# A two-channel convolution beside attention: filter rows loaded one row and one channel per DMA, ten row slots in a ring

## The chip, the cores and the metric

The kernel runs on one core of one Trainium2 chip. A core has a matrix engine (TensorE, PE in the profile, its weight loads PEld), a vector engine (VectorE, DVE), a scalar engine (ScalarE, ACT), GpSimd (POOL) and SyncE (SP), which here does nothing but issue DMAs. Sixteen DMA engines serve the queues of all of them. The metric is the device time of one execution in microseconds (us), lower is better.

## The reference

Two independent blocks share one output of 2048 rows and 1024 columns, in bf16. Block A (columns 0 to 511) is multi-head attention with 32 heads of 16; block B (columns 512 to 1023) is a long convolution over 2048 time steps, a filter for each of 512 channels, between two products.

```
def _A_ref(x, wqkv, wo):                      # x (1, 2048, 512), 32 heads
    qkv = (x @ wqkv) -> q, k, v
    p = softmax(q k^T * 16**-0.5)
    return (p v) @ wo

def _B_ref(q, k, v, shift_k, ssm_k, ssm_D):   # each (1, 2048, 512); ssm_k (512, 2048)
    k_shift = 4-tap causal filter of k along time, by channel
    kv = k_shift * v
    y = causal convolution of kv with ssm_k along time, by channel (there through an FFT)
    y = y + kv * ssm_D
    return q * y

return concatenate([a, b], axis=-1)
```

## The kernel before, in words

The program is written out engine by engine: a planner in Python keeps a time for each engine, takes the next piece of work that fits, and appends instructions to the five engines' lists with the semaphores that each must wait for. Nothing is reordered after that. The backbone is attention in steps T: `emit_qk` puts two or three blocks of scores into PSUM (L546), ScalarE takes their exponential (L557), some blocks go to VectorE instead (L593 to L605), and `pv_step` multiplies the results by V (L639) two steps later. Between these, `emit_bg` fills TensorE's free time with projections and with the convolution.

The convolution runs over 64 octets of channels (`NOCT`), `od` in the code, and an octet over 32 lags (`NLAG`). A lag is four matmuls (L814), one for each pair of channels: the pair's row `c` of the octet holds one channel on partitions 0 to 63 and the other on partitions 64 to 127. The moving operand is a slice of `WR`, ten slots of 128 partitions by 2048 elements. What stands there is a filter row read at a shifting start: partition p of a half takes 2048 elements from element p on of that channel's row, so that one stored row of `kz_scratch` (a padded, reversed copy of the filters in device memory) fills 64 partitions with 4 KB each.

`load_wr` fills the slots, in SP's queue, whenever slots are free. `wr_free` is the list of free slots with the handle that frees each; `wr_slot[x]` tells where item `x` went; `h_wr[x]` is the handle of its landing. Before the change an item is a pair of neighbouring rows in a pair of slots (five pairs, semaphores `d_wr0` to `d_wr4`), and its two halves are loaded by two DMAs of 64 partitions x 2 rows x 2048 elements, 512 KB each. An octet uses two items. At the last lag of an octet `conv_lags` returns its slots and calls `load_wr`, so SP waits there for a matmul (`s_pe`) and then issues the loads of an octet in one go. Six slots are filled at first, after the store of `kz_scratch` (`kz_store`); the other four hold V for the products of k and v until those are done. `emit_bg` starts an octet only when its rows have landed by the planner's reckoning (400 KB a us, 3.6 us ahead of the first).

Of the kernel before, what the change touches and what calls it, by code (L numbers as in the profile page):

```python
# [11 lines left out]
S = 2048  # L12
# [122 lines left out]
def bass_concat_heads__mha_block__ssm_conv_h3__prompt_kernel(  # L135
# [125 lines left out]
    d_outB = [DmaSem(sem(f"d_outB{i}")) for i in range(2)]  # L261
    d_outE = DmaSem(sem("d_outE"))
    d_outA = [DmaSem(sem(f"d_outA{i}")) for i in range(R_A)]
    d_wr = [DmaSem(sem(f"d_wr{i}")) for i in range(R_W // 2)]


    wview = A_wqkv.rearrange("(c p) f -> p c f", p=128)
# [111 lines left out]
    def evac_unit(u, bank, h):  # L379
        kind = u[0]  # L380
        if kind == "q":
            _, qb, o = u
            for par in range(2):
                hh = h_q[(qb, 2 * o + par)] = urgent(
                    lambda e, par=par: e.tensor_scalar(QT[:, qb % 2, 2 * o + par, :], PS[:, bank, :], MASK[:, par:par + 1], None, ALU.mult),  # L385
                    [h, h_mask] + ([h_kzt[0], h_kvm[0]] if qb == 1 else []), us=V512)
        elif kind == "k":
            _, o, sc = u
            c0 = KEYS0 if (o, sc) == (0, 0) else 0
            hh = urgent(lambda e: e.tensor_copy(KTo[:, o, sc * 512 + c0:(sc + 1) * 512], PS[:, bank, c0:512]), [h],  # L390
                        us=(0.335, 0.46) if c0 else V512)
            h_k[(o, sc)] = hh
        elif kind == "kv":
            _, c, i = u
            for p in range(2):
                dst = KV[64 * p:64 * p + 64, i // 4, 4 * (i % 4):4 * (i % 4) + 4, p, 32 * c:32 * c + 32, :].rearrange("p e k c -> p k e c")
                val = VST[64 * p:64 * p + 64, c, i // 4, 4 * (i % 4):4 * (i % 4) + 4, :].rearrange("p e (k c) -> p k e c", c=4)
                src = PS[64 * p:64 * p + 64, bank, :].rearrange("p (e k c) -> p k e c", e=4, c=4)
                h_kvc[c] = hh = urgent(lambda e, dst=dst, src=src, val=val: e.tensor_tensor(dst, src, val, ALU.mult),  # L399
                                       [h, h_vn[2 * c + i // 4], h_kv0], us=V512)  # L400
            kv_n[c] += 1
            if c == 0 and kv_n[0] == 8:
                load_qn(0, [h])
            if sum(kv_n) == 16:
                h_kvm[0] = h
                wr_free.extend([(3, hh), (4, hh)])
                load_wr()
        else:
            _, kt = u
            dst = VAF[:, kt, 0:H * VW].rearrange("p (h e) -> p h e", e=VW)[:, :, 0:DH]  # L410
            src = PS[:, bank, :].rearrange("p (h e) -> p h e", h=H)
            hh = urgent(lambda e: e.tensor_copy(dst, src), [h, h_vaf1], us=V512)  # L412
            h_v[kt] = hh
        bank_free[bank] = hh
# [22 lines left out]
    def kz_store(us):  # L437
        h = dve.op(lambda e: e.tensor_tensor(KZS[:, :, S - 1:S], KZS[:, :, S - 1:S], DSS, ALU.add), [h_kzt[0]], us=us)
        h_kzw[0] = dma(sp, d_kzw, kz_ap.rearrange("(p c) m -> p c m", c=4), KZS, [h, h_kz0], kb=2176)
        load_kt(1, h_kzt[0])  # L440
        wr_free.extend([(i, h_kzw[0]) for i in range(3)])
        load_wr()

    def make_dg(us):
# [339 lines left out]
    wr_slot = {}  # L784

    def load_wr():
        while wr_free and wr_next[0] < 2 * NOCT:
            (i, dep), x = wr_free.pop(0), wr_next[0]
            wr_next[0] += 1
            wr_slot[x] = i  # L790
            for h in range(2):
                row = 256 * (x // NOCT) + 128 * h + 2 * (x % NOCT)
                src = bass.AP(tensor=kz_ap.tensor, offset=kz_ap[row, 0].offset, ap=[[1, 64], [LKZ, 2], [1, S]])
                h_wr[x] = dma(sp, d_wr[i], WR[64 * h:64 * h + 64, 2 * i:2 * i + 2, :], src, [h_kzw[0], dep])

    def load_qn(i, deps):
        h_qn[i] = dma(pool, d_q[0], QN[:, :, :],
# [1 line left out]

    def conv_lags(od, n0, n1):  # L800
        kk = od % 4
        deps = [h_wr[2 * od], h_wr[2 * od + 1], h_kvc[2 * od // NOCT]]
        rows = [2 * wr_slot[2 * od + c // 2] + c % 2 for c in range(4)]
        if kk == 0 and n0 == 0:
            deps.append(bank_free[BGB])

# [12 lines left out]
        h = pe.op(fn, deps, us=(0.06 + 0.055 * (n1 - n0), 0.46 + 0.055 * (n1 - n0)),  # L819
                  run=0.054 * (n1 - n0))  # L820
        if n1 == NLAG:
            wr_free.extend([(wr_slot[2 * od], h), (wr_slot[2 * od + 1], h)])
            load_wr()
            if kk == 3:
                src = PS[:, BGB, :]
                src = bass.AP(tensor=src.tensor, offset=PS[:, BGB, 127:128].offset,
                              ap=[src.ap[0], [128, 4], [-1, 128]])
                hh = urgent(lambda e: e.tensor_copy(YB[:, :].rearrange("p (k i) -> p k i", k=4), src),
                            [h, h_yb.get(od // 4 - 1)], slack=0.3, us=V512)
                bank_free[BGB] = h_ybw[od // 4] = hh  # L830
# [123 lines left out]
    def emit_bg(T):  # L954
# [154 lines left out]
```

## Time and profile before

| | us |
|---|---|
| median of 2 runs | 979.33 |
| lowest, highest | 978.06, 980.59 |
| the profiled execution | 979.65 |
| its span, first to last instruction | 977.8 |

The profiled execution's time is 1.85 us over its span; what lies around the span is not in the trace. Busy shares are averages over a span with three stages: an opening of some 200 us with loads and projections, a middle in which attention and convolution run side by side, and an end after the last octet at 950 us.

### The profile page before, as it was taken

To read this page: it belongs to the slowest core of one execution; us is meant where nothing else is said; L and a number is where in the kernel's file an instruction comes from. 1 tells how busy PE (TensorE), PEld (TensorE's weight loads), DVE (VectorE), ACT (ScalarE), POOL (GpSimd) and SP (SyncE) were. 2 spreads that over 40 slices of the span, in tenths; PEclk is the share of its full clock that TensorE was granted. 3 is DMA by queue.
4 is the path that set the end of the run, shared out by engine and by line. 5 is a ranking of instruction groups with operands and counts; after the bars stand their busy time and mean duration, and the time that the engine had idled before them with its cause. 6 is when DMAs were issued, how large, how long until landed. Compare 5 with 4: busy or idle time off the path is not lost.

```text
span 977.8 us, 29610 instructions
## 1 busy us (share of the span) xinstructions
PE 813.6 (83%) x13388; PEld 329.1 (34%) x13388; DVE 792.9 (81%) x1330; ACT 851.5 (87%) x746; POOL 31.5 (3%) x34
## 2 busy tenths in 40 slices
PE   7988989887887888778888877888798788887877
PEld 2223233433333333333333333333333333332322
DVE  3238899997789898879979877888888889898992
ACT  5998899897889888878979877888898889898897
POOL 7000000000000000000000000000000000000000
PEclk9998799897889899998979888889988989899899
DMA  9950004439878988896878979888877878786502
GB/s 261 244 125 1 1 20 96 104 80 202 187 176 194 218 183 188 183 218 138 183 174 184 220 170 252 189 189 185 180 177 164 182 167 182 179 203 150 131 2 65
DMA packets 68013, 155.14 MB, mean 159 GB/s; under 512 B 31152, under 2 KB 33200, under 8 KB 67504
## 3 DMA queue, kind: packets, MB, share of 16 engines
q1 hardware_dynamic: 62624, 145.12, 67.5%
q0 software_dynamic: 1808, 6.29, 2.3%
q8 instruction: 106, 1.74, 0.8%
q10 hardware_dynamic: 3456, 1.84, 0.7%
q14 instruction: 19, 0.16, 0.1%
HBM read 142.61 MB, written 6.42 MB: 152 GB/s over the span
## 4 chain that ended last, share of the span: by engine, by line
ACT 37%; PE 32%; DVE 20%; issue 9%; SPq 1%; DMA 1%; ACTq 0%
ACT PT L557 37%; PE PS L546 12%; DVE EH L600 8%; PE PS L814 8%; PE PS L639 7%; DVE FX L593 4%; DVE PTD L605 3%; PE PS L1019 1%; PE PS L360 1%; DVE KV L399 1%; PE PS L339 1%; DVE DT L703 1%; DVE QT L385 1%; SPq L222 1%; DMA WR<-in_B_ssm_D_dram 1%
## 5 line engine op out<-in xcount | busy, mean ns | idle before, releaser
L557 ACT ACTIVATE PT<-PS 128x1536 bf16<-128x1536 f32 (+1 forms) x741 | 848.5, 1279 | 113.9 <-PE PS L546 111.6
L546 PE MATMUL PS<-QT,KTo 32*128 32x512 bf16 x2048 | 330.8, 416 | 83.1 <-ACT PT L557 44.1
L814 PE MATMUL PS<-WR,KV 128*30 128x128 bf16 (+8 forms) x8192 | 262.0, 234 | 46.0 <-issue 44.4
L600 DVE SCALAR_TENSOR_TENSOR EH<-EH,FX 128x512 f32<-128x512 f32 x426 | 281.4, 681 | 0.4
L639 PE MATMUL PS<-PT,VAF 128*32 128x512 bf16 x1835 | 222.1, 422 | 14.7 <-issue 8.2
L814 PEld LDWEIGHTS PS<-WR,KV 128*18 128x18 bf16 (+7 forms) x8192 | 175.5, 99 | 150.1 <-issue 117.4
L593 DVE TENSOR_SCALAR FX<-PS 128x512 f32<-128x512 f32 x213 | 146.2, 687 | 60.4 <-PE PS L546 59.8
L546 PEld LDWEIGHTS PS<-QT,KTo 32*128 32x128 bf16 x2048 | 74.7, 92 | 264.1 <-ACT PT L557 176.3
L605 DVE SCALAR_TENSOR_TENSOR PTD<-EH,FX 128x512 uint16<-128x512 f32 x213 | 144.2, 681 | 0.2
L600 DVE SCALAR_TENSOR_TENSOR EH<-FX 128x512 f32<-128x512 uint16 x213 | 142.0, 684 | 0.1
L639 PEld LDWEIGHTS PS<-PT,VAF 128*32 128x32 bf16 x1835 | 50.7, 94 | 151.5 <-issue 132.7
L1019 PE MATMUL PS<-IDN,ZW 128*32 128x512 bf16 (+3 forms) x243 | 81.6, 336 | 5.1 <-issue 5.1
L639 PE MATMUL PS<-PTD,VAF 128*32 128x512 bf16 x213 | 68.7, 432 | 0.0
L703 DVE STREAM_TRANSPOSE DT<-PS 128x512 f32<-128x512 f32 x31 | 22.1, 714 | 31.9 <-PE PS L639 31.6
L412 DVE CAST VAF<-PS 128x512 bf16<-128x512 f32 x16 | 11.1, 691 | 29.2 <-PE PS L368 29.2
L1019 PEld LDWEIGHTS PS<-IDN,ZW 128*32 128x32 bf16 x243 | 24.9, 103 | 9.1 <-issue 9.1
L385 DVE TENSOR_SCALAR QT<-PS,MASK 128x512 bf16<-128x512 f32 x30 | 21.1, 745 | 8.3 <-PE PS L339 8.3
L399 DVE TENSOR_TENSOR KV<-PS,WR 64x512 bf16<-64x512 f32 x32 | 21.9, 686 | 6.1 <-PE PS L360 5.5
L222 POOL DMA_DIRECT2D out_dram<-OUTA x12 | 6.6, 547 | 591.8 <-DVE OUTA L765 591.8
L368 PE MATMUL PS<-WKV,xT 128*128 128x512 bf16 x64 | 19.7, 399 | 4.7 <-DVE VAF L412 4.1
L339 PE MATMUL PS<-xT,WQ 128*128 128x512 bf16 x60 | 21.4, 447 | 1.0 <-DVE QN L847 0.9
L756 PE MATMUL PS<-WKV,OTN 128*128 128x512 bf16 x64 | 20.1, 393 | 1.2 <-DVE OTN L725 1.2
(63 smaller groups left out, 229.6 us busy)
## 6 DMA issues: line engine op xcount, KB each, us to landing
WR<-kz_scratch SPq DMA_DIRECT2D x256, 512.0 KB, 8.7
kz_scratch<-WR SPq DMA_DIRECT2D x1, 2176.0 KB, 8.5
WR<-in_B_v_dram SPq DMA_DIRECT2D x8, 256.0 KB, 6.3
QN<-in_B_q_dram POOLq DMA_DIRECT2D x2, 1024.0 KB, 10.0
out_dram<-QN POOLq DMA_DIRECT2D x2, 1024.0 KB, 9.4
out_dram<-OUTA POOLq DMA_DIRECT2D x12, 128.0 KB, 6.1
QN<-in_B_ssm_k_dram SPq DMA_DIRECT2D x1, 1024.0 KB, 6.1
QT<-in_B_ssm_k_dram SPq DMA_DIRECT2D x1, 1024.0 KB, 8.1
```

The source lines that it names most:

```text
L339: return e.matmul(PS[:, bank, :], lhsT=WQ[:, dc, o * 128:(o + 1) * 128], rhs=xT[:, dc, qb * 512:(qb + 1) * 512], start=(dc == 0), stop=(dc ...
L385: lambda e, par=par: e.tensor_scalar(QT[:, qb % 2, 2 * o + par, :], PS[:, bank, :], MASK[:, par:par + 1], None, ALU.mult),
L399: h_kvc[c] = hh = urgent(lambda e, dst=dst, src=src, val=val: e.tensor_tensor(dst, src, val, ALU.mult), [h, h_vn[2 * c + i // 4], h_kv0], ...
L546: ins = e.matmul(PS[:, bank, :], lhsT=KTo[32 * s:32 * s + 32, g // 2, kt * 128:(kt + 1) * 128], rhs=QT[32 * s:32 * s + 32, qb % 2, g, :], ...
L557: h_exp[T] = act.op(lambda e: e.activation(PT[:, T % R_PT, 0:n * QB], PS[:, banks[0]:banks[0] + n, :].rearrange("p b f -> p (b f)"), ACT.E ...
L593: h_f = urgent(lambda e: e.tensor_scalar(fx, PS[:, bank, :], FIX_ADD, FIX_HI, ALU.add, ALU.min), [h, h_last.get(i - R_FX)], slack=0.6)
L600: st["h"] = dve.op(lambda e: e.scalar_tensor_tensor(eh, src, (A3, A2, A1)[j], frac, ALU.add, ALU.mult), [st["h"], h_last.get(i - R_EH), h_ ...
L605: lambda e: e.scalar_tensor_tensor(out16, eh, A4, fx, ALU.mult, ALU.add),
L639: ins = e.matmul(dst, lhsT=w, rhs=rhs, start=(k == 0), stop=(k == KT - 1), tile_position=(0, 32 * s))
L703: h_t = urgent(lambda e: e.transpose(out=dt, in_=PS[:, pvb(n), :]), [h] + before, slack=0.1, us=(0.63, 0.751))
L814: ins = e.matmul(PS[32 * c:32 * c + 32 - 2 * q, BGB, 128 * kk:128 * kk + w], lhsT=KVF[:, od, lag % 2, 2 * q:32, c], rhs=WR[:, rows[c], w0: ...
L1019: pe.op(lambda e: e.matmul(PS[32 * s:32 * s + 32, pvb(n), 0:128 * k], lhsT=ZW[:, :], rhs=rhs, start=False, stop=False, tile_position=(0, 3 ...
```

## The change

An item is now one row in one slot. There are ten slots with a semaphore each (`d_wr0` to `d_wr9`), an octet uses four items, and an item is loaded by two DMAs of 64 partitions x 2048 elements, 256 KB each. The free list deals in slots: six after the store, four after the products, four at the end of each octet. Rows go to the same places in the same order. The first matmul of an octet takes four landings as its conditions where it took two, and the planner's price of a load is halved (`kb=256`) beside an unchanged price of the issue.

```
@@ -261,7 +261,7 @@
     d_outB = [DmaSem(sem(f"d_outB{i}")) for i in range(2)]
     d_outE = DmaSem(sem("d_outE"))
     d_outA = [DmaSem(sem(f"d_outA{i}")) for i in range(R_A)]
-    d_wr = [DmaSem(sem(f"d_wr{i}")) for i in range(R_W // 2)]
+    d_wr = [DmaSem(sem(f"d_wr{i}")) for i in range(R_W)]
 
 
     wview = A_wqkv.rearrange("(c p) f -> p c f", p=128)
@@ -403,7 +403,7 @@
                 load_qn(0, [h])
             if sum(kv_n) == 16:
                 h_kvm[0] = h
-                wr_free.extend([(3, hh), (4, hh)])
+                wr_free.extend([(i, hh) for i in range(6, R_W)])
                 load_wr()
         else:
             _, kt = u
@@ -438,7 +438,7 @@
         h = dve.op(lambda e: e.tensor_tensor(KZS[:, :, S - 1:S], KZS[:, :, S - 1:S], DSS, ALU.add), [h_kzt[0]], us=us)
         h_kzw[0] = dma(sp, d_kzw, kz_ap.rearrange("(p c) m -> p c m", c=4), KZS, [h, h_kz0], kb=2176)
         load_kt(1, h_kzt[0])
-        wr_free.extend([(i, h_kzw[0]) for i in range(3)])
+        wr_free.extend([(i, h_kzw[0]) for i in range(6)])
         load_wr()
 
     def make_dg(us):
@@ -784,14 +784,17 @@
     wr_slot = {}
 
     def load_wr():
-        while wr_free and wr_next[0] < 2 * NOCT:
+        while wr_free and wr_next[0] < 4 * NOCT:
             (i, dep), x = wr_free.pop(0), wr_next[0]
             wr_next[0] += 1
             wr_slot[x] = i
+            row = 256 * (x // (2 * NOCT)) + x % (2 * NOCT)
             for h in range(2):
-                row = 256 * (x // NOCT) + 128 * h + 2 * (x % NOCT)
-                src = bass.AP(tensor=kz_ap.tensor, offset=kz_ap[row, 0].offset, ap=[[1, 64], [LKZ, 2], [1, S]])
-                h_wr[x] = dma(sp, d_wr[i], WR[64 * h:64 * h + 64, 2 * i:2 * i + 2, :], src, [h_kzw[0], dep])
+                src = bass.AP(tensor=kz_ap.tensor, offset=kz_ap[row + 128 * h, 0].offset, ap=[[1, 64], [1, S]])
+                h_wr[x] = dma(sp, d_wr[i], WR[64 * h:64 * h + 64, i, :], src, [h_kzw[0], dep], kb=256)
+
+    def wr_rows(od):
+        return [h_wr[4 * od + c] for c in range(4)]
 
     def load_qn(i, deps):
         h_qn[i] = dma(pool, d_q[0], QN[:, :, :],
@@ -799,8 +802,8 @@
 
     def conv_lags(od, n0, n1):
         kk = od % 4
-        deps = [h_wr[2 * od], h_wr[2 * od + 1], h_kvc[2 * od // NOCT]]
-        rows = [2 * wr_slot[2 * od + c // 2] + c % 2 for c in range(4)]
+        deps = wr_rows(od) + [h_kvc[2 * od // NOCT]]
+        rows = [wr_slot[4 * od + c] for c in range(4)]
         if kk == 0 and n0 == 0:
             deps.append(bank_free[BGB])
 
@@ -819,7 +822,7 @@
         h = pe.op(fn, deps, us=(0.06 + 0.055 * (n1 - n0), 0.46 + 0.055 * (n1 - n0)),
                   run=0.054 * (n1 - n0))
         if n1 == NLAG:
-            wr_free.extend([(wr_slot[2 * od], h), (wr_slot[2 * od + 1], h)])
+            wr_free.extend([(r, h) for r in rows])
             load_wr()
             if kk == 3:
                 src = PS[:, BGB, :]
@@ -978,8 +981,8 @@
         st["lags"] = min(st["lags"] + min(PACE * st["left"] / left_us, RATE) * (pe.t - st["t"]), CAP)
         st["t"] = pe.t
         left = min(LAGS, int(st["lags"]), int((room(T) - 0.06) / 0.055))
-        while left > 0 and 2 * st["qd"] + 1 < wr_next[0] and kv_n[2 * st["qd"] // NOCT] == 8 \
-                and at(h_wr[2 * st["qd"]], h_wr[2 * st["qd"] + 1]) + WAIT <= pe.t:
+        while left > 0 and 4 * st["qd"] + 3 < wr_next[0] and kv_n[2 * st["qd"] // NOCT] == 8 \
+                and at(*wr_rows(st["qd"])) + WAIT <= pe.t:
             if st["turn"] and st["qd"] % 4 == 3 and st["lag"] + left >= NLAG:
                 left = NLAG - 1 - st["lag"]
                 if left <= 0:
```

On SP's queue the loads stand as follows, before and then after; `x5` means five more of the same, `d_kzw` is the store of the scratch rows, `s_pe` and `s_dve` are TensorE and VectorE.

```order
L222 DMA WR<-kz_scratch 64x2x2048 [waits d_kzw]
L222 DMA WR<-kz_scratch 64x2x2048 x5
L222 DMA WR<-kz_scratch 64x2x2048 [waits s_pe]
L222 DMA WR<-kz_scratch 64x2x2048 x3
L222 DMA WR<-kz_scratch 64x2x2048 [waits s_pe]
L222 DMA WR<-kz_scratch 64x2x2048 x3
```

```order
L222 DMA WR<-kz_scratch 64x2048 [waits d_kzw]
L222 DMA WR<-kz_scratch 64x2048 x11
L222 DMA WR<-kz_scratch 64x2048 [waits s_pe]
L222 DMA WR<-kz_scratch 64x2048 x7
L222 DMA WR<-kz_scratch 64x2048 [waits s_pe]
L222 DMA WR<-kz_scratch 64x2048 x7
```

SP waits at the same places and then issues twice as many DMAs of half the size.

On TensorE this is the place where one octet ends and the next begins, before and then after (L814 and, after the change, L817 are the convolution; L546 scores; L639 the product with V):

```order
L546 MATMUL PS<-QT,KTo 128x512 x2
L639 MATMUL PS<-PT,VAF 32x512 x2
L814 MATMUL PS<-WR,KV 4x128 x4
L814 MATMUL PS<-WR,KV 2x128 x8
L814 MATMUL PS<-WR,KV 32x128 [waits d_wr1,d_wr4]
L814 MATMUL PS<-WR,KV 32x128 x3
L814 MATMUL PS<-WR,KV 32x64 x4
```

```order
L546 MATMUL PS<-QT,KTo 128x512 x2
L639 MATMUL PS<-PT,VAF 32x512 x2
L817 MATMUL PS<-WR,KV 4x128 x4
L817 MATMUL PS<-WR,KV 2x128 x8
L817 MATMUL PS<-WR,KV 32x128 [waits d_wr2,d_wr3,d_wr9,d_wr8]
L817 MATMUL PS<-WR,KV 32x128 x3
L817 MATMUL PS<-WR,KV 32x64 x4
```

The matmuls stand where they stood; the first of an octet has two waits more. On VectorE, ScalarE and GpSimd nothing moves.

## Rows read from the trace of the kernel before

**Rows 1.** Page, part 1: busy us (share of the span) xinstructions.

```profile
PE 813.6 (83%) x13388; PEld 329.1 (34%) x13388; DVE 792.9 (81%) x1330; ACT 851.5 (87%) x746; POOL 31.5 (3%) x34
```

**Rows 2.** Page, part 4: the chain that ended last, share of span.

```profile
ACT 37%; PE 32%; DVE 20%; issue 9%; SPq 1%; DMA 1%; ACTq 0%
```

**Rows 3.** Waits of TensorE, 200 to 920 us: us in total, times, longest us.

```profile
PE PS L814 <- issue: 43.9, 30, 3.1
...
PE PS L546 <- issue: 17.2, 9, 3.9
PE PS L639 <- issue: 8.2, 5, 2.4
PE PS L1019 <- issue: 5.1, 2, 3.7
```

**Rows 4.** Windows: stretch, its length, busy us of each engine, clock, DMA share, GB/s.

```profile
0.00:200.00 200.00, 177.38 (x1739) 60.51 (x1739) 137.19 (x223) 176.14 (x164) 20.72 (x18) 0.90 0.45 104
200.00:920.00 720.00, 592.24 (x11110) 253.28 (x11110) 616.80 (x1038) 623.72 (x538) 9.64 (x15) 0.89 0.83 183
920.00:978.00 58.00, 43.95 (x541) 15.30 (x541) 38.95 (x71) 51.66 (x46) 1.17 (x1) 0.98 0.17 46
```

**Rows 5.** Page, part 3: DMA queue, kind: packets, MB, share of 16 engines.

```profile
q8 instruction: 106, 1.74, 0.8%
```

**Rows 6.** Windows between successive long waits of TensorE (PE, PEld, DVE, ACT, POOL).

```profile
287.82:311.66 23.84, 19.12 (x380) 8.70 (x380) 19.45 (x33) 19.95 (x17) 0.00 (x0) 0.88 0.78 175
311.67:334.86 23.19, 18.15 (x379) 8.14 (x379) 21.50 (x37) 20.67 (x18) 0.56 (x1) 0.99 0.92 200
```

**Rows 7.** Timeline of TensorE: start, us, what, [idle before <-releaser].

```profile
358.07 0.53 PE L814 MATMUL PS<-WR,KV 128*30 128x128 bf16 x16 [1.36 <-issue]
...
366.37 0.23 PE L814 MATMUL PS<-WR,KV 128*8 128x128 bf16 x2 [1.82 <-issue]
```

**Rows 8.** Window from the end of one wait to the next one's start.

```profile
358.08:364.54 6.46, 6.44 (x127) 3.01 (x127) 4.86 (x9) 4.84 (x5) 0.00 (x0) 0.74 0.98 242
```

**Rows 9.** DMA queues from 358.1 to 363.7 us: packets, MB, share.

```profile
q1 hardware_dynamic: 335, 1.24, 88.6%
q0 software_dynamic: 48, 0.13, 8.1%
```

**Rows 10.** DMA queues from 363.7 to 365.1 us.

```profile
q1 hardware_dynamic: 69, 0.27, 96.4%
q8 instruction: 1, 0.02, 5.8%
```

**Rows 11.** Timeline of ScalarE after the wait that ends at 366.37 us.

```profile
367.03 2.37 ACT L557 ACTIVATE PT<-PS 128x1536 bf16<-128x1536 f32 x2 [0.94 <-PE PS L546]
```

**Rows 12.** Waits of ScalarE, whole span.

```profile
ACT PT L557 <- PE PS L546: 111.6, 132, 3.9
```

**Rows 13.** Instructions on tile WR: duration ns min/median/max, first and last start us.

```profile
L814 PE MATMUL PS<-WR,KV x8192: 189/219/315, 144.5 to 950.1; 128*4 128x128 bf16 x15, 128*28 128x128 bf16 x14, 128*18 128x128 bf16 x14, 128*10 128x128 bf16 x14
L222 SPq DMA_DIRECT2D WR<-kz_scratch x256: 573/607/1647, 46.7 to 919.2; - x128
...
L222 SPq DMA_DIRECT2D WR<-in_B_ssm_D_dram x1: 432/432/432, 9.7 to 9.7; - x1
...
DMA to landing us min/median/max: 4.3/8.7/19.0
```

**Rows 14.** Line 814: idle time before it (us, times) until.

```profile
  issue: 161.8, 297
...
  DMA WR<-kz_scratch: 0.2, 1
```

**Rows 15.** Line 118, the waits that stand as instructions: duration ns.

```profile
L118 PEldq EVENT_SEMAPHORE  x309: 51/51/749, 3.5 to 949.5; - x155
```

**Rows 16.** Timeline of SP's queue, one octet's loads.

```profile
356.11 2.82 SPq L222 DMA_DIRECT2D WR<-kz_scratch  x4
```

**Rows 17.** Waits of SP's queue, whole span.

```profile
SPq L222 <- PE PS L546: 354.0, 26, 111.5
```

**Rows 18.** Window in which four row loads stand in line.

```profile
327.00:331.00 4.00, 3.95 (x67) 1.48 (x69) 2.91 (x6) 3.98 (x4) 0.56 (x1) 1.00 1.03 213
```

More of the change, by code (lines that the diff above doesn't have):

```diff
@@ L263, in bass_concat_heads__mha_block__ssm_conv_h3__prompt_kernel @@
     d_outA = [DmaSem(sem(f"d_outA{i}")) for i in range(R_A)]
-    d_wr = [DmaSem(sem(f"d_wr{i}")) for i in range(R_W // 2)]
+    d_wr = [DmaSem(sem(f"d_wr{i}")) for i in range(R_W)]
     wview = A_wqkv.rearrange("(c p) f -> p c f", p=128)
@@ L405, in evac_unit @@
                 h_kvm[0] = h
-                wr_free.extend([(3, hh), (4, hh)])
+                wr_free.extend([(i, hh) for i in range(6, R_W)])
                 load_wr()
@@ L440, in kz_store @@
         load_kt(1, h_kzt[0])
-        wr_free.extend([(i, h_kzw[0]) for i in range(3)])
+        wr_free.extend([(i, h_kzw[0]) for i in range(6)])
         load_wr()
@@ L786, in load_wr @@
     def load_wr():
-        while wr_free and wr_next[0] < 2 * NOCT:
+        while wr_free and wr_next[0] < 4 * NOCT:
             (i, dep), x = wr_free.pop(0), wr_next[0]
@@ L790, in load_wr, with wr_rows @@
             wr_slot[x] = i
+            row = 256 * (x // (2 * NOCT)) + x % (2 * NOCT)
             for h in range(2):
-                row = 256 * (x // NOCT) + 128 * h + 2 * (x % NOCT)
-                src = bass.AP(tensor=kz_ap.tensor, offset=kz_ap[row, 0].offset, ap=[[1, 64], [LKZ, 2], [1, S]])
-                h_wr[x] = dma(sp, d_wr[i], WR[64 * h:64 * h + 64, 2 * i:2 * i + 2, :], src, [h_kzw[0], dep])
+                src = bass.AP(tensor=kz_ap.tensor, offset=kz_ap[row + 128 * h, 0].offset, ap=[[1, 64], [1, S]])
+                h_wr[x] = dma(sp, d_wr[i], WR[64 * h:64 * h + 64, i, :], src, [h_kzw[0], dep], kb=256)
+    def wr_rows(od):
+        return [h_wr[4 * od + c] for c in range(4)]
     def load_qn(i, deps):
@@ L801, in conv_lags @@
         kk = od % 4
-        deps = [h_wr[2 * od], h_wr[2 * od + 1], h_kvc[2 * od // NOCT]]
-        rows = [2 * wr_slot[2 * od + c // 2] + c % 2 for c in range(4)]
+        deps = wr_rows(od) + [h_kvc[2 * od // NOCT]]
+        rows = [wr_slot[4 * od + c] for c in range(4)]
         if kk == 0 and n0 == 0:
@@ L821, in conv_lags @@
         if n1 == NLAG:
-            wr_free.extend([(wr_slot[2 * od], h), (wr_slot[2 * od + 1], h)])
+            wr_free.extend([(r, h) for r in rows])
             load_wr()
@@ L980, in emit_bg @@
         left = min(LAGS, int(st["lags"]), int((room(T) - 0.06) / 0.055))
-        while left > 0 and 2 * st["qd"] + 1 < wr_next[0] and kv_n[2 * st["qd"] // NOCT] == 8 \
-                and at(h_wr[2 * st["qd"]], h_wr[2 * st["qd"] + 1]) + WAIT <= pe.t:
+        while left > 0 and 4 * st["qd"] + 3 < wr_next[0] and kv_n[2 * st["qd"] // NOCT] == 8 \
+                and at(*wr_rows(st["qd"])) + WAIT <= pe.t:
             if st["turn"] and st["qd"] % 4 == 3 and st["lag"] + left >= NLAG:
```

## The prediction

> **What bounds the kernel now.** I read the share of busy time first, then the chain of waits, then the waits of TensorE, and last the DMA queues around one wait. ScalarE is busy for 87% of the span, TensorE for 83% and VectorE for 81% [rows 1]: no engine is full, and three are close. The chain that ended last runs through all three and has 9% of the span, 88 us, as "issue", time in which the engine waited for nothing that the profile shows [rows 2]. That is the odd entry, and it has a place. From 200 to 920 us TensorE's matmuls stood idle for "issue" in 30, 9, 5 and 2 cases, 43.9 + 17.2 + 8.2 + 5.1 = 74.4 us [rows 3]. From 0 to 200 us and from 920 us on, the same view lists no such wait. What sets the middle apart is the DMA share: 0.45, 0.83 and 0.17 in the three stretches [rows 4].
>
> The long ones are TensorE's sequencer waiting for instructions. The queue of kind "instruction" moved 106 packets, 1.74 MB [rows 5]; TensorE has 13388 matmuls, as many weight loads [rows 1] and 309 semaphore waits [rows 15], and 27085 / 106 = 255.5, so one packet brings a block of 256. Between the ends of successive long waits stand 380 matmuls + 380 loads, then 379 + 379 [rows 6]; with some 8 to 10 semaphore waits that is 768 = 3 x 256 each time. One case in full: a wait of 1.36 us ends at 358.07, the next, of 1.82 us, at 366.37 [rows 7], and in between TensorE ran 127 + 127 instructions in 6.46 us [rows 8], one block. In the 5.6 us from 358.1 the engines moved 1.24 MB for SP's queue and no instruction packet [rows 9]; that packet came in the next 1.4 us [rows 10], and 1.3 us after that TensorE went on. So the next block, wanted at 358.1, stood 5.6 us behind filter rows that SP had already handed over. ScalarE felt it: it idled 0.94 us before its next exponential [rows 11], and 111.6 us in the run for TensorE's scores [rows 12].
>
> Filter rows themselves are not late. Of the idle time ahead of the convolution's matmuls and loads, 161.8 us is "issue" and 0.2 us is the landing of a row [rows 14]. A change that only brings rows earlier has nothing to win.
>
> **The change, part by part.** The order of instructions on TensorE, VectorE, ScalarE and GpSimd is the same as before; so is the number of row slots in flight (ten rows, of which an octet frees four). Three things differ.
>
> *Twice the DMAs on SP, half as large.* SP issues 512 instead of 256. One takes 607 ns [rows 13], four take 2.6 to 2.8 us in a row [rows 16]. If a half one takes SP as long, an octet's eight take 8 x 0.65 = 5.2 us; the shortest issue of a small DMA was 432 ns [rows 13], which would make it 3.8 us. SP carries nothing else then: it waited 354.0 us for one kind of matmul alone [rows 17], and behind these loads stand only the two last output stores. The engines need 512 KB / 213 GB/s = 2.46 us for an old DMA [rows 18], 9.84 us for an octet's four, so SP stays ahead at 0.65 us against 1.23 us for a half, and the last row lands when it did. That is costed at nothing; the cover is the engines' queue, and where it ran dry an octet's last row would come up to 2.6 us later.
>
> *What a fetch finds ahead of it.* The first data move about 4.3 - 2.46 = 1.8 us after the issue (the fastest landing [rows 13] less its transfer). Before, SP has queued 6.0 us of transfers 1.6 us into a hand-over and 9.0 us at 2.6 us. After, by the same reckoning, it has queued 3.0 us and 4.1 us (4.9 less 0.8 drained), and 6.4 us at 5.2 us, where both are equal again. The fetch above waited 5.6 us with more than that queued, so I take 6 us as the most that a fetch waits. The wait then falls by 3.0 us at 1.6, 1.9 at 2.6, 0.6 at 4 and nothing from 5.2 us on: some 1.35 us over 5.2 us of an octet of (950.1 - 144.5) / 64 = 12.6 us [rows 13], 0.56 us a fetch on average. From 200 to 920 us there are 2 x 11110 / 255.5 = 87 fetches [rows 4], so the upper end is 49 us. The lower end is nothing: a late fetch is mostly one that asks when the queue is already deep, and there 6 us stay 6 us. Half of the fetches (46 of 87) end in an "issue" wait, which leaves 25 us; those sit at the deep end, where the saving is under 1 us, so I take **15 us** off the 74.4. A TensorE wait passes on nearly whole, since the chain counts 88 us of "issue".
>
> *More waits on TensorE.* The first matmul of an octet waits for four row semaphores, not two. The built program has 375 semaphore-wait instructions on TensorE instead of 311: 64 x 51 ns [rows 15] = 3.3 us at most, nothing at least where the array is still draining earlier matmuls. I take **3.3 us**, since a wait stands in the same queue as all matmuls behind it. They also shift the blocks' borders by up to 64 instructions, which deals the late fetches anew; 46 waits of 1.6 us on average that differ by about 1 us each make that some 7 us either way (an estimate from [rows 3]).
>
> *More completions on the DMA engines.* 256 more DMAs, 16 increments each. No row prices one apart; it lies inside the 2.46 us. Between nothing and 0.2 us each (a twelfth of that) an octet's 9.84 us grow by at most 0.8 us, still under 12.6; rows are late for 0.2 us in the whole run [rows 14], so I take nothing and 5 us as the far end.
>
> The sum against the profiled execution (979.65 us, its span 977.8; the median is 979.33, 0.3 us less, which I ignore): 979.65 - 15 + 3.3 = **968 us**.
>
> **The rivals.** *A, nothing gained:* the fetch's wait is set by a depth that the engines take in ahead, deep enough that halving the DMAs leaves it full. For it: 5.6 us in the case above, with two of SP's old DMAs and more ahead. Against it: the queue does fill more slowly. Time: 979.65 + 3.3 = 983, 979 to 986.
>
> *B, nearly all fetch waits go:* the engines change queues only at the end of a DMA's share, and a fetch needs some two such changes before its data flow. A half DMA then halves the wait, 5.6 to 2.8 us; with the 1.4 us of the packet and 1.3 us behind it that is 5.5 us, inside the 6.46 us that TensorE takes for a block [rows 8]. Time: 979.65 - 74.4 + 3.3 = 909, and up to 945 where half stays. Against it: 1.24 MB are 2.4 old DMAs, more than one change would let past [rows 9]. The Trainium skill ("DMA: Bandwidth & Descriptors", Queues, rings and completion order) states such a rule: an engine drains a whole packet of some 9 to 17 descriptors from one ring before it turns to the next. By that rule an old DMA's share would be one such packet, and a fetch should wait for one; the trace shows over two, so it agrees at best in part.
>
> *C, slower:* the eight half DMAs hold the engines longer than an octet lasts, because a part of the 2.46 us belongs to the DMA and not to its bytes. It decides from 12.6 / 8 = 1.57 us a half DMA, 0.34 us over the half of 2.46. At 1.7 us an octet lasts 13.6 us, one more for some 62 of them: 979.65 + 62 + 3.3 = 1045. Against it: 16 engines at a share of 1.03 while four DMAs stand in line [rows 18], with no hole in which such a part could lie. [...]
>
> **How the numbers follow.** The forecast has 0.52, between 955 and 978; A 0.25, B 0.15 (905 to 945), C 0.05, and 0.03 lies between B and the forecast. The range runs from 945 to 986: it leaves out most of B, and C. Two per cent, about what a measurement of this kernel can tell from no change, is 19.6 us: under 959.7 us lie B and a fifth of the forecast, 0.25; over 998.9 us lies C, 0.05; the rest is 0.70.
>
> **What would show it.** Right: "issue" ahead of TensorE's matmuls from 200 to 920 us falls from 74 to about 60 us, its waits still three-block or one-block distances apart, the row loads' wait stays near nothing, SP's 512 issues take some 0.6 us each, and semaphore waits rise to 373 records. A shows the same 74 us; B shows under 30; C shows TensorE waiting for the landing of rows, and the DMA share near 1 throughout. The prediction is wrong if the fetch's wait hangs on the number of DMAs ahead rather than on their bytes, or if rows read one at a time run at another rate than rows read in pairs.

## The result, and the profile after

The changed kernel takes 895.44 us (median of two runs, 894.57 and 896.31) against 979.33: a ratio of 0.9143, 95% interval 0.908 to 0.9207. The forecast of 968 us and its range of 945 to 986 both miss it; it lies even below the 905 to 945 us of rival B. The profiled execution took 896.31 us, 83.3 us less than the one before. Executions of one kernel spread by up to 3%, the longer ones at a lower granted clock: medians below are of all runs, while ratios, and what a pause of TensorE costs, go by the runs within 1.5% of the fastest.

The first lines are the page's part 1 and part 4 of the changed kernel (busy us, share, instructions; then the chain that ended last), to be held against [rows 1, 2].

```profile
PE 766.8 (86%) x13388; PEld 312.7 (35%) x13388; DVE 789.3 (88%) x1330; ACT 842.3 (94%) x746; POOL 31.6 (4%) x34
...
ACT 48%; DVE 27%; PE 15%; DMA 5%; issue 3%; SPq 2%; ACTq 0%
```

ScalarE is now busy for 94% of the span, and "issue" has 3% of the chain instead of 9%. The line to stop at is TensorE's: the same 13388 matmuls were busy for 766.8 us instead of 813.6 [rows 1]. The granted clock of the span rose from 0.900 to 0.956, and that accounts for it: 813.6 x 0.900 = 732 and 766.8 x 0.956 = 733.

The waits of TensorE from 200 to 920 us (us in total, times, longest), beside [rows 3]:

```profile
PE PS L546 <- ACT PT L557: 59.6, 190, 0.7
PE PS L817 <- issue: 11.5, 9, 4.2
...
PE PS L817 <- DMA WR<-kz_scratch: 1.6, 5, 0.4
```

ScalarE's wait for scores over the whole span, beside [rows 12]:

```profile
ACT PT L557 <- PE PS L546: 38.5, 63, 3.9
```

With 0.7 us on line 546, "issue" has fallen from 74.4 us in 46 cases to 12.2 in 11. TensorE now waits longest, in total, for ScalarE, and ScalarE waits for TensorE's scores 38.5 us instead of 111.6. The stretches (columns as in [rows 4]):

```profile
0.00:200.00 200.00, 176.05 (x1689) 57.89 (x1689) 135.38 (x220) 174.35 (x162) 20.74 (x18) 0.89 0.44 104
200.00:840.00 640.00, 548.75 (x11201) 240.46 (x11199) 618.23 (x1048) 619.06 (x543) 9.67 (x15) 0.97 0.87 207
840.00:895.00 55.00, 41.98 (x503) 14.38 (x503) 35.71 (x64) 48.88 (x43) 1.17 (x1) 1.00 0.12 35
```

The first 200 us are nearly as they were (1689 matmuls and 1739). Nearly all of the gain is in the stretch with the filter rows, which does as many matmuls as that of [rows 4] (11201 and 11110) in 80 us less, at a granted clock of 0.97 instead of 0.89. The instruction queue moved what it moved before [rows 5]:

```profile
q8 instruction: 106, 1.74, 0.9%
```

The instructions on tile WR (answering to [rows 13]):

```profile
L817 PE MATMUL PS<-WR,KV x8192: 190/219/314, 146.5 to 866.9; 128*4 128x128 bf16 x16, 128*24 128x128 bf16 x14, 128*28 128x128 bf16 x14, 128*18 128x128 bf16 x14
L222 SPq DMA_DIRECT2D WR<-kz_scratch x512: 444/597/2297, 46.6 to 837.2; - x171
...
DMA to landing us min/median/max: 3.4/6.1/12.7
```

TensorE's semaphore waits that stand as instructions (line 118, as [rows 15]):

```profile
L118 PEldq EVENT_SEMAPHORE  x373: 51/51/51, 3.5 to 866.2; - x187
```

An issue of half the bytes takes SyncE as long as before (597 ns against 607), as reckoned, and a load lands 6.1 us after it instead of 8.7.

**How deep the queue is when a fetch is asked for.** The prediction argued with one case; the records give all. All 33 "issue" waits of the kernel before that are over 0.7 us fall on the same place in TensorE's instructions, one in 256, and each ends 1.3 to 1.8 us after the end of the instruction packet that brings the block it stands before. For 81 successive blocks that begin while rows are loaded (from 246 to 895 us before, from 247 to 814 us after) I counted, from the records of instructions and packets, (1) the 4 KB row packets that SyncE had handed over and that were not finished when TensorE entered a block, divided by 16 engines, and (2) the time from there to the end of the instruction packet that brings the next block. Medians (and the values that a quarter of the blocks exceed): before, 21.3 (25.4) packets ahead and 6.4 (7.4) us; after, 13.9 (16.7) packets and 3.8 (4.8) us. Without row loads (e3 and e14 below) the same time is about 1.4 us. TensorE took 7.1 us on average for a block in the changed kernel. Before, 39 of the 81 fetches met over 22 packets; after, two did.

### The profile page after: what moved, and what is told of

Read it like the earlier page. It is cut to its first block, busy times and chain, and to the rows that moved or that the text cites. A ratio compares the mean times of both kernels' runs of the same rounds, so it can differ in the third digit from the quotient of the medians.

```text
span 894.6 us, 29930 instructions
## 1 busy us (share of the span) xinstructions
PE 766.8 (86%) x13388; PEld 312.7 (35%) x13388; DVE 789.3 (88%) x1330; ACT 842.3 (94%) x746; POOL 31.6 (4%) x34
## 4 chain that ended last, share of the span: by engine, by line
ACT 48%; DVE 27%; PE 15%; DMA 5%; issue 3%; SPq 2%; ACTq 0%
ACT PT L557 48%; DVE EH L600 12%; PE PS L546 6%; DVE FX L593 5%; DVE PTD L605 4%; DMA WR<-kz_scratch 4%; PE PS L639 3%; PE PS L817 2%; SPq L222 2%; DVE KV L399 2%; DVE QT L385 1%; DMA WR<-in_B_ssm_D_dram 1%; PE PS L360 1%; DVE DT L703 1%; PE PS L339 1%
## 5 line engine op out<-in xcount | busy, mean ns | idle before, releaser
L557 ACT ACTIVATE PT<-PS 128x1536 bf16<-128x1536 f32 (+1 forms) x741 | 839.2, 1341 | 39.8 <-PE PS L546 38.5
L546 PE MATMUL PS<-QT,KTo 32*128 32x512 bf16 x2048 | 312.8, 397 | 90.9 <-ACT PT L557 64.6
L817 PE MATMUL PS<-WR,KV 128*30 128x128 bf16 (+8 forms) x8192 | 239.2, 223 | 14.8 <-issue 11.5
L639 PE MATMUL PS<-PT,VAF 128*32 128x512 bf16 x1835 | 209.4, 402 | 6.2 <-DVE DT L703 5.0
L817 PEld LDWEIGHTS PS<-WR,KV 128*18 128x18 bf16 (+7 forms) x8192 | 164.4, 96 | 104.9 <-issue 66.9
L546 PEld LDWEIGHTS PS<-QT,KTo 32*128 32x128 bf16 x2048 | 73.4, 91 | 268.9 <-ACT PT L557 217.0
L639 PEld LDWEIGHTS PS<-PT,VAF 128*32 128x32 bf16 x1835 | 49.7, 93 | 131.7 <-issue 113.6
L1022 PE MATMUL PS<-IDN,ZW 128*32 128x512 bf16 (+3 forms) x243 | 77.6, 319 | 0.1
L639 PE MATMUL PS<-PTD,VAF 128*32 128x512 bf16 x213 | 62.7, 394 | 0.0
L703 DVE STREAM_TRANSPOSE DT<-PS 128x512 f32<-128x512 f32 x31 | 22.0, 711 | 17.9 <-PE PS L639 17.4
L339 PE MATMUL PS<-xT,WQ 128*128 128x512 bf16 x60 | 19.4, 412 | 1.3 <-DVE QN L850 1.1
```

The costliest lines, as they stand in the source:

```text
L339: return e.matmul(PS[:, bank, :], lhsT=WQ[:, dc, o * 128:(o + 1) * 128], rhs=xT[:, dc, qb * 512:(qb + 1) * 512], start=(dc == 0), stop=(dc ...
L546: ins = e.matmul(PS[:, bank, :], lhsT=KTo[32 * s:32 * s + 32, g // 2, kt * 128:(kt + 1) * 128], rhs=QT[32 * s:32 * s + 32, qb % 2, g, :], ...
L557: h_exp[T] = act.op(lambda e: e.activation(PT[:, T % R_PT, 0:n * QB], PS[:, banks[0]:banks[0] + n, :].rearrange("p b f -> p (b f)"), ACT.E ...
L639: ins = e.matmul(dst, lhsT=w, rhs=rhs, start=(k == 0), stop=(k == KT - 1), tile_position=(0, 32 * s))
L703: h_t = urgent(lambda e: e.transpose(out=dt, in_=PS[:, pvb(n), :]), [h] + before, slack=0.1, us=(0.63, 0.751))
L817: ins = e.matmul(PS[32 * c:32 * c + 32 - 2 * q, BGB, 128 * kk:128 * kk + w], lhsT=KVF[:, od, lag % 2, 2 * q:32, c], rhs=WR[:, rows[c], w0: ...
```

## The experiments

Every kernel keeps TensorE's order of matmuls and weight loads. An octet's hand-over is the stretch in which SyncE issues its loads. The theories: **P**, the pace at which SyncE hands over an octet's loads decides how much a fetch finds ahead; **S**, the size of one load decides (rival B's mechanism); **R**, rows read singly rather than in pairs have a gain of their own; **C**, a wait of TensorE also costs its clock afterwards. **D**, formed after the first four, is P put in general: what decides is how many row packets stand ahead of a fetch, whatever keeps them few.

The kernels without pauses, except e11, in one table. "Handed over" is the median time from the first to the last issue of an octet's loads, "ahead" and "fetch" the two medians just defined, "issue" the waits of TensorE's matmuls from 200 to 920 us without the groups whose longest is 0.3 us or less (such stand there without loads too). These, and the time under "profiled", are of the profiled execution; "time" is the median of all runs. The traces of e1 and e2 lack 43 matmul records, so their blocks are counted by the weight loads, which are complete (counted by all records, as the expectation of e5 has them, they give 18.4 and 17.4 packets, 4.9 and 4.7 us). The first two rows of times are from the runs of the result; the others had the kernel before beside them at 976.5 to 981.0 us.

| kernel | load KB | handed over us | ahead | fetch us | issue us | profiled us | time us | ratio (95%) |
|---|---|---|---|---|---|---|---|---|
| before | 512 | 1.9 | 21.3 | 6.4 | 74.4 | 979.7 | 979.3 | |
| changed | 256 | 4.7 | 13.9 | 3.8 | 12.2 | 896.3 | 895.4 | 0.914 (0.908, 0.921) |
| e1 | 512 | 3.4 | 17.7 | 5.8 | 56.6 | 967.8 | 966.3 | 0.982 (0.975, 0.990) |
| e13 | 512 | 5.1 | 15.0 | 4.9 | 31.6 | 911.5 | 916.6 | 0.936 (0.929, 0.943) |
| e2 | 256 pairs | 3.7 | 16.2 | 5.6 | 51.8 | 939.6 | 943.3 | 0.957 (0.949, 0.964) |
| e10 | 256 pairs | 4.7 | 14.9 | 4.9 | 31.3 | 919.1 | 920.1 | 0.937 (0.931, 0.943) |
| e12 | 256 pairs | 5.3 | 12.3 | 4.3 | 15.2 | 886.0 | 901.4 | |
| e7 | 256 | capped | 11.7 | 3.2 | 1.2 | 876.9 | 875.9 | 0.895 (0.890, 0.899) |
| e6 | 128 | 8.0 | 8.0 | 2.3 | 0 | 888.1 | 879.2 | 0.897 (0.890, 0.903) |
| e5 | 512 | capped | 8.2 | 2.9 | 1.4 | 960.9 | 959.7 | 0.976 (0.969, 0.982) |
| e3 | none | | | | 0 | 875.3 | 872.2 | 0.888 (0.881, 0.894) |

**e1_pace: the old loads, handed over more slowly.** Before, with one-element loads to a spare tile behind each load of an octet, two, two, two and none.

```
 h_wr[x] = dma(sp, d_wr[i], WR[64 * h:64 * h + 64, 2 * i:2 * i + 2, :], src, [h_kzw[0], dep])
+tiny(2 if h == 0 or x % 2 == 0 else 0)
```

> The kernel before, its 512 KB DMAs unchanged, with six tiny DMAs (one element each) put between an octet's four loads in SP's queue, so that SP hands the four over in some 5 us instead of 2.7 us. Theory P (pace: a fetch waits behind the bytes that SP has handed over when it asks, and the halves hand them over half as fast): TensorE's issue waits fall from 74 us to under 35, time 900 to 935 us. Theory S (share: an engine serves a DMA's whole share before the fetch's, so the size of one DMA counts): issue waits stay at 60 to 80 us, time 968 to 985. Theory R (rows read one at a time are read otherwise than pairs): as S.

966.26 us (959.23 to 972.35), in neither interval. A small gain, so P looked refuted. But the hand-over had become 3.4 us and not 5 (a one-element load takes SyncE only some 0.3 us): the dose was half of what was meant, and the verdict on P was put off to e13.

**e2_quarters: small loads, pairs of rows.** Before, with each load cut across the partitions.

```
-for h in range(2):
+for h in range(4):
-    ... ap=[[1, 64], [LKZ, 2], [1, S]]   into 64 partitions
+    ... ap=[[1, 32], [LKZ, 2], [1, S]]   into 32 partitions, kb=256
```

> The kernel before with row pairs, slots and waits unchanged, but each DMA cut by partitions: 32 partitions x 2 rows, 256 KB, 512 DMAs in all. P and S: as the changed kernel, 888 to 905 us, issue waits under 25 us. R (single rows make the gain): 965 to 985 us, issue waits near 74 us.

943.3 us (933.2 to 952.61), in the hole between the expectations. The issue explains part of it. This is SyncE's line on tile WR:

```profile
L222 SPq DMA_DIRECT2D WR<-kz_scratch x512: 302/427/1792, 46.7 to 879.0; - x171
```

A load of 32 partitions is issued in 427 ns where 64 partitions take 597, at the same 256 KB: the first and the last of an octet's eight are 3.7 us apart, not 4.7. So this kernel too differs from the changed one in its pace.

**e3_noload: what the loads cost in all.** Before, where a slot is filled once and later loads into it are left out (the later octets compute with the first rows).

```
+if i in filled and filled[i] != x:
+    ...                           # the planner's times as before
+    h_wr[x] = (Unloaded(), x)     # no load, no wait for it
+    ...
+    continue
+filled[i] = x
```

> The kernel before with only the first filling of each slot loaded; all later row loads are left out, so the convolution runs on old rows and its output is not the reference's. TensorE's order is unchanged. All theories of the fetch: issue waits from 200 us on go to under 5 us. Time 870 to 895 us if the fetch waits and what follows from them are the whole price of the loads; under 870 if the loads cost something else too.

872.2 us (869.14 to 875.26), with no "issue" wait over 0.3 us from 200 to 920 us and a granted clock of 1.00 from 200 to 840 us (columns as in [rows 4]):

```profile
200.00:840.00 640.00, 544.62 (x11440) 241.75 (x11459) 636.51 (x1082) 635.36 (x560) 9.65 (x15) 1.00 0.05 12
```

All of the stage's long "issue" waits come from the row loads, and loading rows costs the kernel before 107 us (979.3 - 872.2), much more than the 74.4 us of waits. The changed kernel had won back 84 of them.

**e9_pauses: the price of a wait.** The changed kernel with 31 pauses of TensorE, each waiting for five short GpSimd fills that start when TensorE comes to it.

```
+if 200 <= T < 696 and T % 16 == 8:
+    pause()
```

> The changed kernel with 31 pauses of TensorE, one every 16 attention steps from step 208 on: TensorE waits there for GpSimd, which clears an unused tile five times (some 2 us). No DMA is added. Theory C (a wait costs TensorE's clock too): time grows by clearly more than the pauses themselves, 31 x 2 = 62 us, to 965 to 985 us, and the granted clock falls from 0.956 towards 0.90. Rival (only the waits count, the clock follows something else): at most 62 us more, 935 to 958 us, clock near 0.95.

980.94 us (964.76 to 994.19; ratio to before 0.9919, 0.9867 to 0.9971). The profiled execution (986.36 us) has 61.2 us of pauses in 31 places. The fastest four runs, up to 975.56, take 971 us on average, 76 us more than the changed kernel, at a granted clock of 0.90 instead of 0.956. C holds, but row loads and fetches were still in play; e14 repeats it without them.

**e5_bcap2: few under way, old size.** Before, with SyncE waiting for the landing of the load two places ahead; four waits an octet on TensorE as in the changed kernel.

```
+ld = dma(sp, d_wr[2 * i + h], ..., held=flight[-2] if len(flight) >= 2 else None)
```

> The kernel before with its four 512 KB loads an octet, but SyncE hands over a load only once the load two places ahead of it has landed, so that at most two (1 MB, 16 packets on each DMA engine) are ever under way; each half of a slot has a semaphore of its own, which gives TensorE the four waits per octet of the changed kernel. Theory D (what decides is how many packets stand ahead of an instruction fetch when TensorE asks for it: in the median 21 on an engine in the kernel before, 18 with tiny loads between, 17 with 256 KB pairs, 14 in the changed kernel, with a fetch taking 6.4, 4.9, 4.7 and 3.8 us): the deep end is cut off, 890 to 925 us, with under 30 us of issue waits. Theory S (the size of one DMA decides, the queue's depth doesn't): 965 to 985 us, issue waits 60 us or more. A third outcome, that rows land late because SyncE waits: over 985 us, with waits of TensorE for WR.

959.73 us (952.69 to 961.21), outside all three intervals. The waits show why: D's "issue" waits and the third outcome's late rows came together. TensorE's waits, 200 to 920 us:

```profile
PE PS L822 <- DMA WR<-kz_scratch: 73.1, 32, 5.7
PE PS L549 <- ACT PT L560: 41.5, 143, 0.7
```

The "issue" waits are gone (1.4 us) with 512 KB loads, since only 8.2 packets are ahead of a fetch; S expected 60 us or more of them. What the cap gave it took back, 73.1 us, as rows that land late.

**e6_eighths: 128 KB loads.** The changed kernel with each load cut across the partitions (and the planner's price of an issue halved for them, which keeps the order).

```
-for h in range(2):
+for h in range(4):
-    ... ap=[[1, 64], [1, S]]   into 64 partitions, kb=256
+    ... ap=[[1, 32], [1, S]]   into 32 partitions, kb=128
```

> The changed kernel with each 256 KB load cut once more into two of 128 KB (32 partitions of one row), 1024 loads instead of 512, 16 hand-overs an octet. Both S (a smaller share of one DMA stands ahead of a fetch) and D (16 hand-overs of 0.4 to 0.6 us take 6.4 to 9.6 us of an octet's 11.3, so fewer packets stand in the queue) expect the rest of the issue waits to go: 872 us is what is left with no loads at all, so 875 to 892 us, issue waits under 6 us of the 12 left, granted clock of the convolution over 0.98. The rival is that SyncE becomes the bound: at over 0.7 us for a hand-over 16 of them take the whole octet, rows land late, TensorE waits for WR, and the time is 905 us or more.

879.18 us (876.25 to 888.08): the rest of the "issue" waits is gone, as both theories said. TensorE waited 7.6 us for rows from 200 to 920 us; SyncE's 16 issues take 8.0 us from the first to the last, of the 9.7 us from one octet's first load to the next (medians), so they come near their limit, but don't reach it.

**e10_quarters_pace: pairs at the pace of the changed kernel.** e2 with a one-element load behind every second load.

```
 h_wr[x] = dma(sp, d_wr[i], WR[32 * h:32 * h + 32, 2 * i:2 * i + 2, :], src, [h_kzw[0], dep], kb=256)
+if h % 2 == 0:
+    tiny(1)
```

> The kernel with 256 KB loads of pairs of rows (32 partitions of two rows), and four one-element loads put between an octet's eight, so that their hand-over takes about 5 us instead of 3.8, as in the changed kernel (4.8). It differs from the changed kernel only in that a load reads two rows of half as many partitions, and that slots are freed in pairs. Theory D (size and pace together set how many packets stand ahead of a fetch): 895 to 920 us, as the changed kernel. Theory R (single rows are what made the other half of the gain, by the order in which they are read or freed): 935 to 950 us, as with the pairs of 256 KB without the one-element loads (943).

920.05 us (917.01 to 925.17). Just over the upper edge of D's interval and below R's: the pace alone has brought half of the distance from 943 to 895. The loads went out two at a time, 0.35 us apart, then 0.79 us; 14.9 packets ahead.

**e11_rows512: single rows of 512 KB.** The changed kernel with one load for both channels of a row.

```
+src = bass.AP(..., ap=[[128 * LKZ, 2], [1, 64], [1, S]])
+h_wr[x] = dma(sp, d_wr[i], WR[:, i, :], src, [h_kzw[0], dep])
```

> The changed kernel with one load for both channels of a row: 512 KB as in the kernel before (128 partitions of one row), four an octet, ten row slots, four waits an octet. Theory D: the hand-over of four takes 2 us as before, the packets ahead of a fetch are as before, 960 to 985 us. Theory R (single rows, not the size): 900 to 945 us. Theory S: as D, 960 to 985.

2751.75 us (2745.97 to 2756.4), which none of them had. It tests nothing about rows: what it shows is another thing. First TensorE's waits over the span:

```profile
PE PS L816 <- DMA WR<-kz_scratch: 1782.8, 63, 32.5
```

Then SyncE's line on tile WR, and SyncE's DMA queue from 1000 to 1100 us (packets, MB, share of 16 engines):

```profile
L222 SPq DMA_DIRECT2D WR<-kz_scratch x256: 482/9892/17373, 46.7 to 2671.4; - x128
```

```profile
q1 hardware_dynamic: 1289, 5.20, 12.8%
```

A share of 12.8% of 16 engines is the time of two engines, and 512 KB in the 9.9 us of one issue are 53 GB/s; the trace doesn't tell the engines apart. The source's outermost dimension is 2, where it was 64 or 32 before, and the row loads of the other kernels filled the engines. That this dimension is the cause was not tested by itself.

**e13_pace12: the old loads, still more slowly.** e1 with three one-element loads behind each.

```
-tiny(2 if h == 0 or x % 2 == 0 else 0)
+tiny(3)
```

> The kernel before, 512 KB loads, with three one-element loads behind each of an octet's four: some 1.9 us apart, 5.7 to 6.5 us from the first to the last (1.9 us in the kernel before; 3.4 with six one-element loads, which gave 966). Theory D: the queue that a fetch meets falls to 14 to 16 packets on an engine in the median, 925 to 950 us, though a 512 KB load leaves 8 packets on an engine where one of 256 KB leaves 4. Theory S, that the size of a load counts by itself: 958 to 970 us, no more gained than with six.

916.63 us (911.0 to 928.88): below the whole of S's interval, and just under D's. The kernel with loads of the old size, unchanged in rows, slots and waits, takes some 60 us less than the kernel before beside it (976.5) when they are handed over in 5.1 us. TensorE's waits, 200 to 920 us:

```profile
PE PS L828 <- issue: 22.8, 19, 2.6
PE PS L549 <- issue: 7.6, 5, 5.1
...
PE PS L828 <- DMA WR<-kz_scratch: 2.7, 8, 0.6
```

Beside e10 this is the cleanest pair of the study: 15.0 and 14.9 packets ahead, 31.6 and 31.3 us of issue waits, 916.6 and 920.1 us, with 512 KB in the one and 256 KB in the other. S, that the size of a load decides, falls.

**e12_quarters_pace8: pairs, evenly spaced.** e2 with a one-element load behind each load (the cut below is against e10).

```
-if h % 2 == 0:
-    tiny(1)
+tiny(1)
```

> The 256 KB loads of row pairs (32 partitions of two rows) with a one-element load behind each of an octet's eight, instead of four: evenly spaced, some 0.75 us apart, 5.3 to 6.3 us for an octet (the changed kernel: 0.64 apart, 4.8 us; with four one-element loads: two loads 0.35 us apart and then 0.79). Theory D, depth: no more packets stand ahead of a fetch than in the changed kernel (at most about 14 on an engine in the median), 885 to 905 us. Theory R, that reading single rows has a gain of its own: it stays at 912 to 930, near the 920 of four one-element loads.

Four runs: 886.01, the profiled one, to which the 12.3 packets and 15.2 us of issue waits belong, then 901.38, 901.49 and 907.99. No interval is given to so wide a spread, but three of four lie in D's interval and none in R's: pairs of rows come to the changed kernel's 895 on either side, at a like depth of queue (12.3 and 13.9). R falls.

**e7_cap6: the changed kernel, capped.** SyncE waits, before a row's two loads, for those of the row three places ahead.

```
 h_wr[x] = dma(sp, d_wr[i], WR[64 * h:64 * h + 64, i, :], src, [h_kzw[0], dep], kb=256,
+              held=h_wr.get(x - 3) if h == 0 else None)
```

> The changed kernel, in which SyncE hands over a row's two loads only once those of the row three places ahead have landed: at most six loads of 256 KB (24 packets on an engine) under way. Theory D: only the deepest few of the queues that fetches meet are cut (the long waits of the changed kernel are five, 9.3 us, and its tail reaches 32 packets), 880 to 895 us, issue waits under 8 us. Against it: SyncE's wait delays rows as it did with two 512 KB loads (73 us of waits for WR), then 900 us or more with waits of TensorE for WR over 15 us.

875.89 us (872.64 to 887.43), better than expected and the fastest of the study: 0.8947 of the kernel before (0.8901 to 0.8992), and near the 872 of no loads at all. Part 1 of its page, and TensorE's waits from 200 to 920 us:

```profile
PE 746.1 (85%) x13388; PEld 307.4 (35%) x13388; DVE 787.3 (90%) x1330; ACT 838.2 (96%) x746; POOL 31.1 (4%) x34
```

```profile
PE PS L821 <- DMA WR<-kz_scratch: 5.0, 2, 4.5
...
PE PS L821 <- issue: 1.2, 1, 1.2
```

Late rows stay at 5.0 us, where e5 had 73.1; six loads of 256 KB keep as much in flight as three of 512 KB, not two.

**e14_noload_pauses: the price of a wait, alone.** e3 (later rows left out as there) with e9's pauses.

```
+if 200 <= T < 696 and T % 16 == 8:
+    pause()
```

> The kernel without the row loads behind the first filling of each slot (872 us; the rows of the later octets are left out, so the convolution reads the first rows again), with 31 pauses of TensorE, each waiting for five short GpSimd fills (2.0 us each in the changed kernel with the same pauses, 61 us in all, which made that kernel 85 us longer). Theory C, a pause costs itself and then a stretch at the lower of TensorE's two clocks: 872 + 61 + 15 to 30 = 948 to 963 us, with 15 or more stretches of 3 to 7 us at half clock that begin behind a pause, where the kernel without pauses has none in the convolution. Without C: 872 + at most 61, so up to 933 us, less what ScalarE's own waits take in, and a granted clock of 0.97 or more.

967.2 us (959.04 to 973.86); the fastest three runs, up to 972.9, take 964.5 on average, just over C's interval and 92 us above the 872.2 of e3. The 31 pauses have these waits:

```profile
PE PS L649 <- POOL PAT L1061: 39.6, 20, 2.6
...
PE PS L835 <- POOL PAT L1061: 15.7, 8, 2.2
...
PE PS L766 <- POOL PAT L1061: 1.9, 1, 1.9
```

With two more of 1.9 they are 61.0 us. Around one of them, windows (columns as in [rows 4]) and the timeline of TensorE:

```profile
510.00:517.90 7.90, 7.02 (x121) 2.48 (x118) 7.90 (x14) 7.73 (x8) 0.00 (x0) 1.00 0.01 2
517.90:519.90 2.00, 0.01 (x3) 0.00 (x1) 2.00 (x5) 1.83 (x2) 1.51 (x5) 1.00 0.00 0
519.90:521.00 1.10, 1.07 (x30) 0.45 (x33) 0.80 (x2) 0.09 (x1) 0.00 (x0) 1.00 0.00 0
521.00:524.40 3.40, 3.40 (x63) 1.29 (x55) 2.42 (x4) 2.97 (x3) 0.00 (x0) 0.50 0.02 5
524.40:530.00 5.60, 4.94 (x136) 2.40 (x128) 4.78 (x9) 5.45 (x6) 0.00 (x0) 1.00 0.00 0
```

```profile
517.52 0.39 PE L556 MATMUL PS<-QT,KTo 32*128 32x512 bf16 x3
519.93 0.59 PE L649 MATMUL PS<-PT,VAF 128*32 128x512 bf16 x5 [2.01 <-POOL PAT L1061]
...
521.32 0.61 PE L556 MATMUL PS<-QT,KTo 32*128 32x512 bf16 x3
```

TensorE stands for 2.0 us at full clock, works on for 1.1 us, and then runs 3.4 us at a granted clock of 0.50, the lower of its two levels (1.2 of 2.4 GHz), in which a score matmul takes 0.61 us instead of 0.39. Not every pause does this: behind 20 of the 31 such a stretch begins within 2 us of TensorE's going on (or up to 0.5 us before it), behind 11 none does. The pauses alone, with hardly any DMA, took the granted clock of the run from 0.975 to 0.901.

## Why the prediction was wrong, step by step

**The place and the cause: right.** The "issue" waits are instruction fetches behind filter rows. e3 without the loads has none, and the seven kernels without a cap and with loads of 256 KB or more order themselves by the packets ahead of a fetch: 21.3, 17.7, 16.2, 15.0, 14.9, 13.9 and 12.3 packets go with 980, 968, 940, 912, 919, 896 and 886 us of the same executions, where 15.0 and 14.9 are one depth within the spread of runs. One reading was off: the opening does list an "issue" wait on the convolution, of 0.5 us.

**Twice the DMAs on SP, costed at nothing: right, and it was the gain.** An issue takes 597 ns, and eight of them 4.8 us where 5.2 were reckoned; waits for landings cost 1.6 us in the stage. The part said that SP stays ahead of the engines, and it does, but by less, which is what the fetch feels.

**What a fetch finds ahead, 15 us: the step that failed.** Measured, the waits fell by 74.4 - 12.2 = 62 us, more than even the upper bound of 49. Three things in it were mis-sized.
- The average saving on a fetch was put at 0.56 us. Over the 81 fetches it fell from 5.69 to 3.88 us, by 1.8.
- "Those sit at the deep end, where the saving is under 1 us" is wrong at its root. The time that a quarter of the fetches exceed fell from 7.4 to 4.8 us, by 2.6. The sum let the saving shrink from 1.9 us at 2.6 us into a hand-over to nothing at 5.2. Sorted by when they were asked for, fetches of the first 2.6 us fell from 6.5 to 3.2 us on average, those from 2.6 to 5.2 us from 7.0 to 4.7, the later ones from 4.4 to 3.8. Moreover 43 of the 81 fell in the first 5.2 us, both before and after, where an even spread over 12.6 us would have put 33. The sum also counted a load as ahead of the fetch from its issue, though the same part had 1.8 us from the issue to the first data. If only loads issued at least 1 us before are counted, 34 of 81 fetches met 19 packets or more before, and one after. That this lag explains the saving late in a hand-over is argued, not shown.
- It took the same 0.56 us off every late wait. A wait is only what a fetch takes beyond its block: with some 1.5 us from the packet's end to TensorE's going on, a median fetch of 6.4 us is late for a block of 7 us, and one of 3.8 us, or even 4.8, is not. Half of the fetches were late; a shift of some 2 us leaves few.

**"Passes on nearly whole": too little.** A wait costs more than its length. e14's pauses cost 92 us for 61.0, e9's 76 for 61.2, so 1.2 to 1.5 us for each. For the 62 us of waits that went, 77 to 94 us follow from that (an estimate); the change brought 84. In the trace, TensorE's span fell by 977.8 - 894.6 = 83.2 us, of which 46.8 are busy time of the same matmuls (813.6 to 766.8) and the rest idle time. That the chain counted 88 us of "issue" showed the wait and hid the clock, though [rows 4] had it: 0.89 in the stage with the waits and 0.98 behind it.

**More waits on TensorE, 3.3 us: no sign of them.** The 373 records came. No run prices them apart; but e7, with four waits an octet and late rows besides, lies 4 us above the kernel without loads, which waits for no later row, so there is little room for them.

**More completions, nothing: holds.** With 1024 loads (e6) the kernel takes 879 us, and the engines move 207 GB/s from 200 to 840 us there as with 512.

**The rivals.** A, the same 74 us of "issue", is out. B has the size of the result, under 30 us of "issue" and 909 us forecast, and the wrong mechanism: it gave the halving of one load's share as the cause, and e13 gains some 60 of the 84 us with no load halved, and e5 loses its "issue" waits with none halved. By the rule that B named, in the Trainium skill ("DMA: Bandwidth & Descriptors", Queues, rings and completion order), one packet of descriptors of another ring, typically some 9 to 17 of them, would go ahead of a fetch. Here, with over 22 ahead, 19.6 of the profile's 4 KB packets an engine were served first in the median, more than two of the old loads (8 an engine each), so a load's share is not what a fetch waits for: the depth counts, up to some 20. How many of the profile's packets make one packet in the Trainium skill's sense no run shows. C, more time held by each DMA, is out in the kernel itself; its place, rows that land late, is what e5 ran into.

What stays open: why about 20 packets an engine are served ahead of a fetch and hardly more (23 at most before and 22 after), and whether the waits for rows in e6 (7.6 us) come from SyncE alone.

## What to carry to other kernels

Where an engine that is nearly full shows "issue" waits only in stages with busy DMA queues, count what the bulk loads have put ahead of an instruction fetch, and keep that queue shallow: by pacing, smaller loads or a cap on the loads in flight, whichever still brings the data in time (six loads of 256 KB gave 876 us, two of 512 KB gave 960). Reckon a fetch against the time that its block runs: one that comes in time costs nothing, however long it took. And price a stall of TensorE of some two microseconds with the slow stretch that often follows it, here 1.2 to 1.5 times its length in all.

## What the runs showed of the hardware that was not expected

- Stalls of 1.9 to 2.6 us in a busy stage are often followed by the half clock: behind 20 of e14's 31 pauses a stretch of 3.4 to 13.7 us at that level begins within 2 us of the pause's end or shortly before it. e14 has 26 such stretches between 200 and 930 us, where e3 without the pauses has none from 200 to 840; the kernel before has 32 in the run with 198 us in all, the changed kernel 10 with 80 us.
- SyncE's time for an issue hardly follows the bytes where loads are issued back to back: in the median 607 and 597 ns for 64 partitions of two rows and of one, 427 and 422 ns for 32 partitions (e2 and e6). The shortest do differ: 573, 444 and 302 ns for 512 KB, for 256 KB into 64 partitions, and for 32 partitions.
- A load whose source has an outermost dimension of 2 moved 53 GB/s and took the time of two of 16 engines, 12.8% (e11); which engines, and whether the dimension is the cause, was not tested.
